# Attention beside an FFN on one core: 21 of 56 FFN1 tiles made during gelu and read from the score banks

## The chip, the cores and the metric

The kernel runs on one core of a Trainium2 chip. The time is the device time of one execution in microseconds (us); the median of several executions is compared. A core has a matrix engine (TensorE, PE), a vector engine (VectorE, DVE), an activation engine (ScalarE, ACT), a general one (GpSimd, POOL) and a queue engine (SyncE, SP), which here starts nearly all DMA transfers. Each engine works through its own list of instructions in order and waits for others by semaphores. PSUM, where matmuls write, has eight banks of 128 x 512 fp32.

## The reference

```python
x = A_x                                  # 1 x 2048 x 448
xn = _layernorm(x, axis=-1)
s = _A_ref(xn, A_wqkv, A_wo)             # attention, 16 heads of 28, softmax over 2048 keys
g = _silu(_B_ref(xn, B_w1, B_b1, B_w2, B_b2))
return x + s * g

def _B_ref(x, w1, b1, w2, b2):           # FFN, 448 -> 1792 -> 448
    h = jnp.einsum("bsd,df->bsf", x, w1) + b1
    h = _gelu(h)                         # tanh form
    return jnp.einsum("bsf,fd->bsd", h, w2) + b2
```

## The kernel before

Queries are cut into four chunks of 512 (c), heads into four groups of four (g). A block b = 4g + c is one group of heads over one chunk of queries. It has 64 score tiles of 128 keys x 512 queries, so there are 1024 tiles, numbered m. Four heads sit in four strips of 32 rows, so the score matmuls of several heads run beside each other in the array.

Six PSUM banks form the ring of scores; of the other two, `acc` gathers the weighted sums (P times V) and `misc` is the one spare bank that everything else shares, one user at a time. From block 1 on, tiles are made in units of three (in block 0, of two): `p_scores` (matmuls, line 1011) fills three banks, `p_exps` (ScalarE, line 1038) turns them into probabilities P with one instruction, and the other three banks are filled meanwhile. `p_pv` (line 1137) multiplies P with V.

Some tiles do not go to ScalarE. They are called late: their exp is computed by VectorE with a polynomial, tile by tile from the ring (line 1065), then in pairs of tiles with five instructions (`p_exp2`, lines 1089 to 1096), and they join the weighted sum when they are ready. `COUNTS` gives the number of late tiles of each of the blocks 1 to 14, and `OFFS` their places and pairing; a late tile is always the third of its unit, so that the unit's exp has two tiles.

The FFN runs beside this. FFN1 has 4 x 14 = 56 tiles of 128 x 512, each four matmuls (line 916) into the spare bank, and VectorE adds b1 while it moves the tile to `h` in SBUF (line 929). When all 56 are done, `p_gelu` puts four gelu instructions of 14 tiles each into ScalarE's list (line 941), between two loads of the activation table; scores and exps stand still for that time. FFN2 (line 959, 14 matmuls for each of 16 tiles), silu by tanh (line 973) and the output projection (line 1226) follow beside the later blocks, again over the spare bank.

The order of each engine's instructions is fixed when the program is built. A planner runs all these processes against estimated durations. Each step is a task with an engine, what it reads and writes, a duration and a priority (a lower number goes first). The planner takes the task that can start earliest, and among those within 0.1 us the one of best priority; the list of each engine is the order in which its tasks were taken. The semaphore waits follow from reads and writes. A process can wait for a condition on the plan (`"until"`) or for a free bank (`"bank"`).

Inputs are loaded through SP's queue at the start: x, the weights, b1 (line 572, 128 x 14 elements), b2, and w1. `constants` clears the padding: `xn` is 448 columns wide, padded with zeros to 512, and rows 448 to 511 of `w1` are zero (line 492).

Of the kernel before, what the change touches and what calls it, by code (L numbers as in the profile page):

```python
# [8 lines left out]
ALU = mybir.AluOpType  # L9
# [10 lines left out]
C = 4  # L20
# [11 lines left out]
OFFS = {2: ((0,), (21,)), 3: ((0, 9), (30,)), 4: ((0, 9), (21, 33)), 5: ((0, 9), (18, 27), (39,)),  # L32
        6: ((0, 9), (18, 27), (33, 39)), 7: ((0, 6), (12, 21), (27, 33), (39,))}
COUNTS = (5, 5, 4, 5, 4, 5, 4, 4, 4, 6, 6, 6, 4, 3)
for _b in range(1, NBLK - 1):
    _m = 64 * _b + 4
    while (_m - 64) % UB != UB - 1:
        _m += 1
    for _o in OFFS[COUNTS[_b - 1]]:
        _ms = tuple(_m + x for x in _o)  # L40
        LATE.update(_ms)
        for _k in _ms:
            PAIR[_k] = _ms
# [3 lines left out]
for _m in list(range(0, 64, 2)) + list(range(64, MTOT, UB)):  # L47
    _ms = list(range(_m, _m + (2 if _m < 64 else UB)))
    _b0 = _m % 4 if _m < 64 else (_m - 64) % NRING
    _na = len([m for m in _ms if m not in LATE])  # L50
    if _p + _na > NP:
        _p = 0
    UNITS.append((_ms, _ms[:_na], _b0, _p))
    for _k, m in enumerate(_ms):
        UOF[m] = len(UNITS) - 1
        RB[m] = _b0 + _k
        RPREV[m] = _last.get(RB[m])
        _last[RB[m]] = m
        if _k < _na:
            PB[m] = _p + _k  # L60
            PPREV[m] = _plast.get(PB[m])
            _plast[PB[m]] = m
    _p += _na
NU = len(UNITS)
# [5 lines left out]
PV_START = 8  # L70
SEM = 0.07
# [25 lines left out]
class _Kernel:  # L97
# [164 lines left out]
    def alloc(self):  # L262
# [28 lines left out]
        self.b1s = sb("b1s", [128, FT], bf)  # L291
        self.b1c = sb("b1c", [128, FT], f32)
# [48 lines left out]
        self.b_b1, self.b_b1c, self.b_b2 = B(), B(), B()  # L341
# [27 lines left out]
        self.s_x2 = [self.sem("s_x2%d" % q) for q in range(4)]  # L369
        self.s_x0b, self.s_wqk1 = self.sem("s_x0b"), self.sem("s_wqk1")  # L370
# [3 lines left out]
    def schedule(self):  # L374
# [28 lines left out]
        K.b1_done = False  # L403
        K.gelu_done = False
        self.constants()
# [9 lines left out]
        K.spawn(K.p_late(), 0)  # L415
        o = 1.0
# [23 lines left out]
        f1 = deque((c, ft) for c in range(C) for ft in range(FT))  # L440
        for c in range(C):
            for _ in range(6):
                K.spawn(K.p_f1(*f1.popleft()), nxt())
            K.spawn(K.p_k(2, c), nxt())
            K.spawn(K.p_q(2, c), nxt())
# [5 lines left out]
        K.spawn(K.p_gelu(), 0)  # L451
        for c in range(C):
            for t in range(4):
                K.spawn(K.p_f2(c, t), nxt())
            K.spawn(K.p_silu(c), nxt())
# [10 lines left out]
    def constants(self):  # L466
# [3 lines left out]
        def f(eng):  # L470
            eng.memset(K.epsc[:, :], LN_EPS)
            eng.memset(K.dum[:, :], 1.0)
            eng.memset(K.ones[:, :], 1.0)
            eng.memset(K.E_sb[:, :, :], 0.0)
            eng.memset(K.stg[64:128, 3, :, :, :], 0.0)
            pad = lambda w: w.rearrange("p k (h e) -> p (k h) e", e=32)[:, :, DH:32]
            eng.memset(pad(K.wq[:, :, :]), 0.0)
            eng.memset(pad(K.wk[:, :, :]), 0.0)
            eng.memset(pad(K.wsq), 0.0)
            return eng.memset(K.xn[:, :, :, D:512], 0.0)  # L480
        e(DVE, f, writes=[K.b_pads], dur=1.6)

        def late_pads():
            yield ("until", lambda: K.b_xnT[0][1].tw is not None)

            def f(eng):
                eng.memset(K.wv[64:128, 3, :], 0.0)
                eng.memset(K.wv[0:64, 3, D:WS], 0.0)
                return eng.memset(K.wv[:, 0:3, D:WS], 0.0)
            yield _Task(DVE, f, [], [K.b_wvpad], 0.4, 0.05, 1)  # L490
            yield ("until", lambda: K.ln_done == 2 * C)
            yield _Task(DVE, lambda eng: eng.memset(K.w1[64:128, 3, :], 0.0), [], [K.b_w1pad], 0.8, 0.05, 4)
        K.spawn(late_pads(), 3)
# [52 lines left out]
    def loads(self):  # L546
# [23 lines left out]
        def f(eng):  # L570
            with K.nc.allow_non_contiguous_dma(reason="tiny bias load"):
                return eng.dma_start(K.b1s[:, :], K.B_b1.rearrange("(ft p) -> p ft", p=128))
        K.dma(SP, f, K.s_w["b"], writes=[K.b_b1], land=20)
        ld(K.b2b[:, :], K.B_b2.partition_broadcast(128), K.s_w["b"], [K.b_b2], 20)
        K.b_b1.w = K.b_b2.w
# [333 lines left out]
    def p_f1(self, c, ft):  # L909
        K = self  # L910
        bank, tok = yield ("bank", lambda: K.ready(K.b_xnT[c] + [K.b_w1, K.b_w1pad, K.b_b1]) and K.stg_done == 2 and K.norms_done)
        for k in range(2):
            def f(eng, k=k):
                ins = None
                for kt in (2 * k, 2 * k + 1):
                    ins = eng.matmul(bank, K.w1[:, kt, ft * 128:(ft + 1) * 128], K.xnT[:, kt, c * 512:(c + 1) * 512],  # L916
                                     start=(kt == 0), stop=(kt == KT - 1))
                return ins
            yield _Task(PE, f, [K.b_w1, K.b_w1pad, K.b_xnT[c][k]], [tok], 0.5, 0.12)
        if not K.b1_done:  # L920
            K.b1_done = True
            yield _Task(DVE, lambda eng: eng.tensor_copy(K.b1c[:, :], K.b1s[:, :]), [K.b_b1], [K.b_b1c], 0.17)
        dst = K.h[:, c, ft * 512:(ft + 1) * 512]
        wr = [K.b_hf[c][ft]]
        if c == 3:
            for x in K.b_xn:
                for y in x:
                    wr[0].r += y.r
        yield _Task(DVE, lambda eng: eng.tensor_scalar(dst, bank, K.b1c[:, ft:ft + 1], None, op0=ALU.add),  # L929
                    [tok, K.b_b1c], wr, 0.75, 0.0, 2)  # L930
        K.banks.append((bank, tok))
        K.n_f1 += 1

    def p_gelu(self):
        K = self
        yield ("until", lambda: K.n_f1 == C * FT and K.ready([b for r in K.b_hf for b in r], 0.5))
        for c in range(C):
            hv = K.h[:, c, :]

            def f(eng, hv=hv):  # L940
                return eng.activation(hv, hv, ACTF.Gelu_apprx_tanh)  # L941
            yield _Task(ACT, f, K.b_hf[c], [K.b_h[c]], 6.15 + (1.3 if c == 0 else 0), 0.0, -1)
        K.prog[ACT].append(lambda eng: eng.preload_act_table_set("exp_and_others"))
        K.tE[ACT] += 1.3
        for b in K.b_fsb + K.b_sig:
            b.w = K.b_w1.w
            b.r = list(K.b_w1.r) + [K.b_w1pad.w]
        K.gelu_done = True

    def p_f2(self, c, t):  # L950
        K = self
        bank, tok = yield ("bank", lambda: K.ready([K.b_h[c], K.b_w2]) and (c < 2 or K.g_done[c - 2]))
# [44 lines left out]
    def p_scores(self):  # L997
        K = self
        for u in range(NU):
# [23 lines left out]
            if len(ms) == 3 and not K.ring6:  # L1023
                yield ("until", lambda: K.taken == 2)
                K.ring6 = True
            yield ("until", lambda: all(RPREV[m] is None or K.ring_rel[RPREV[m]] for m in ms))
# [3 lines left out]
    def p_exps(self):  # L1030
        K = self
        for u in range(NU):
# [11 lines left out]
            K.exp_m = UNITS[u][0][-1]  # L1044
# [4 lines left out]
    def p_late(self):  # L1049
# [5 lines left out]
        for u in range(NU):  # L1055
            for m in UNITS[u][0]:
# [13 lines left out]
                if m == PAIR[m][-1]:  # L1070
                    K.spawn(K.p_exp2(PAIR[m], i), m)

# [31 lines left out]
    def p_pv(self):  # L1104
# [5 lines left out]
        for q in range(MTOT // 4):  # L1110
# [6 lines left out]
            for m, k, half in list(K.late_ready):  # L1117
                hole = (4 * q + m % 4) in LATE and all(m % 4 != x[0] % 4 for x in late)
                if m // 64 == b and (end or len(K.late_ready) - len(late) > 3 or (hole and K.ready([K.b_pl[k]]))):
# [23 lines left out]
            def fall(eng, fl=fl):  # L1143
                ins = None
                for f in fl:
# [3 lines left out]
                        lambda: 1.2 if K.exp_u - K.pv_u > 4 else 6)  # L1149
# [167 lines left out]
```

## Time and profile before

| | |
|---|---|
| median of 7 runs | 499.02 us (497.91 to 500.77) |
| the profiled execution | 500.8 us, span of its instructions 499.0 us |
| mean granted TensorE clock | 0.958 of full |
| ScalarE busy | 475.4 us, 95% of the span |
| TensorE busy | 418.5 us, 84% |
| VectorE busy | 387.9 us, 78% |
| exps on ScalarE | 352 instructions |
| FFN1 moves on VectorE | 56, mean 747 ns |
| first and last start of gelu | 325.3 and 343.5 us |

How to read it: a group's line gives source line, engine, operation, output and input, shapes and count, then the busy time and the mean duration of one in ns, then how long the engine sat idle just before such instructions and what ended that. Durations of neighbours on an engine overlap a little, so the pitch from start to start is what counts in a sum. A row of a table by stretches gives, for each engine, its busy time and number of instructions, then the granted TensorE clock as a share of full, the DMA share and the GB/s. Four matmuls into one tile are shown as one row with x4.

### The profile page before, as it was taken

What the parts mean: (1) busy time and instruction counts of PE and PEld (TensorE: products, weight loads), DVE (VectorE), ACT (ScalarE), POOL (GpSimd) and SP (SyncE); (2) the same over time, 40 slices, a digit from 0 to 9 for tenths busy, and PEclk for the clock granted to TensorE, in tenths of its full rate; (3) what the DMA queues carried; (4) which work ended last, traced back from release to release, by engine and by line L of the source; (5) the groups of instructions that cost most, each with busy time, mean ns of one, the idle gap of its engine ahead of it and who ended that gap; (6) DMA issues with size and microseconds to landing.
All of it is one profiled execution on the core that took longest, in us unless ns stands there. A gap on an engine that the chain in (4) does not pass through costs nothing.

```text
span 499.0 us, 8625 instructions
## 1 busy us (share of the span) xinstructions
PE 418.5 (84%) x3486; PEld 140.2 (28%) x3519; DVE 387.9 (78%) x545; ACT 475.4 (95%) x382; POOL 83.7 (17%) x91
## 2 busy tenths in 40 slices
PE   6999789886998888888788888756899999998884
PEld 4442223221221222222222222211233333322342
DVE  7744998888688968997886969993297999678454
ACT  5998999999999999999999999999799999999994
POOL 6571112041210212121101001041000102010100
PEclk9998999999888999999989999985799999999999
DMA  8500000000000000001300000000001001102110
GB/s 238 146 17 19 0 1 1 0 1 3 0 1 0 1 1 0 2 1 20 111 0 1 1 1 1 1 0 0 0 2 38 2 0 37 39 0 71 43 49 30
DMA packets 10088, 11.00 MB, mean 22 GB/s; under 512 B 3456, under 2 KB 8704, under 8 KB 10048
## 3 DMA queue, kind: packets, MB, share of 16 engines
q1 hardware_dynamic: 9904, 10.21, 6.9%
q8 instruction: 28, 0.46, 0.4%
q10 hardware_dynamic: 144, 0.23, 0.1%
q14 instruction: 12, 0.10, 0.1%
HBM read 8.61 MB, written 1.84 MB: 21 GB/s over the span
## 4 chain that ended last, share of the span: by engine, by line
PE 36%; ACT 31%; issue 18%; DVE 11%; POOL 3%; DMA 1%; ACTq 0%; DVEq 0%; POOLq 0%
ACT P L1038 30%; PE ring L1011 9%; PE misc L959 7%; PE acc L1137 6%; PE misc L916 6%; PE misc L671 3%; DVE h L929 1%; POOL rlo L1202 1%; DVE x_sb L1065 1%; DVE kT L1090 1%; POOL rhi L1201 1%; ACT w L973 1%; DVE kT L682 1%; DVE kT L1089 1%; PE misc L1226 1%
## 5 line engine op out<-in xcount | busy, mean ns | idle before, releaser
L1038 ACT ACTIVATE P<-ring 128x1536 bf16<-128x1536 f32 (+1 forms) x352 | 435.3, 1433 | 11.2 <-PE ring L1011 10.3
L1011 PE MATMUL ring<-qT,kT 32*128 32x512 bf16 (+1 forms) x1216 | 139.2, 355 | 42.4 <-ACT P L1038 38.3
L1137 PE MATMUL acc<-P,vaug 128*32 128x512 bf16 (+1 forms) x1151 | 96.9, 355 | 1.0 <-ACT P L1038 0.4
L1011 PEld LDWEIGHTS ring<-qT,kT 32*128 32x128 bf16 x1216 | 36.9, 91 | 159.6 <-ACT P L1038 137.8
L916 PE MATMUL misc<-xnT,w 128*128 128x512 bf16 x208 | 61.6, 399 | 4.4 <-issue 1.8
L929 DVE TENSOR_SCALAR h<-misc,b1c 128x512 bf16<-128x512 f32 x56 | 41.8, 747 | 24.0 <-PE misc L916 23.7
L1201 POOL CAST rhi<-rc 128x512 bf16<-128x512 f32 x15 | 15.3, 1017 | 242.6 <-DVE rc L1197 216.7
L959 PE MATMUL misc<-w,h 128*128 128x448 bf16 x224 | 53.4, 364 | 2.0 <-DVE qT L852 0.9
L1065 DVE TENSOR_SCALAR x_sb<-ring 128x512 int32<-128x512 f32 x65 | 44.6, 686 | 8.9 <-PE ring L1011 8.4
L857 POOL TENSOR_TENSOR qsq<-qT 128x512 bf16<-128x512 bf16 x15 | 23.3, 1554 | 131.5 <-DVE qT L852 125.2
L1137 PEld LDWEIGHTS acc<-P,vaug 128*32 128x32 bf16 x1151 | 25.5, 94 | 56.9 <-issue 50.1
L959 PEld LDWEIGHTS misc<-w,h 128*128 128x128 bf16 x224 | 17.9, 99 | 27.5 <-issue 14.0
L916 PEld LDWEIGHTS misc<-xnT,w 128*128 128x128 bf16 x224 | 15.9, 100 | 32.0 <-issue 15.4
L941 ACT ACTIVATE h<-h 128x7168 bf16<-128x7168 bf16 x4 | 24.4, 6164 | 0.0
L671 PE MATMUL misc<-xnT,wq 128*128 128x512 bf16 x58 | 18.5, 432 | 5.8 <-DVE qT L862 3.6
L1202 POOL TENSOR_TENSOR rlo<-rc,rhi 128x512 bf16<-128x512 f32 x15 | 22.1, 1470 | 1.2
L1094 DVE SCALAR_TENSOR_TENSOR kT<-kT 128x1024 f32<-128x1024 f32 (+1 forms) x17 | 21.7, 1278 | 0.2
L1090 DVE SCALAR_TENSOR_TENSOR kT<-kT 128x1024 f32<-128x1024 f32 (+1 forms) x17 | 21.2, 1250 | 0.4
L1092 DVE SCALAR_TENSOR_TENSOR w<-w 128x1024 f32<-128x1024 f32 (+1 forms) x18 | 21.2, 1179 | 0.2
L964 DVE TENSOR_TENSOR w<-misc,b2b 128x448 bf16<-128x448 f32 x16 | 9.9, 621 | 14.3 <-PE misc L959 14.3
L1090 DVE SCALAR_TENSOR_TENSOR w<-w 128x1024 f32<-128x1024 f32 (+1 forms) x18 | 20.6, 1145 | 0.4
L1094 DVE SCALAR_TENSOR_TENSOR w<-w 128x1024 f32<-128x1024 f32 (+1 forms) x18 | 20.8, 1153 | 0.1
(135 smaller groups left out, 408.3 us busy)
## 6 DMA issues: line engine op xcount, KB each, us to landing
h<-in_A_x_dram SPq DMA_DIRECT2D x4, 448.0 KB, 3.3
w<-in_B_w_dram SPq DMA_DIRECT2D x1, 1568.0 KB, 7.4
x_sb<-in_A_x_dram SPq DMA_DIRECT2D x3, 448.0 KB, 5.8
w<-in_B_w_dram SPq DMA_DIRECT2D x1, 1344.0 KB, 7.8
out_dram<-h SPq DMA_DIRECT2D x6, 224.0 KB, 1.9
h<-in_A_wqkv_dram SPq DMA_DIRECT2D x3, 168.0 KB, 5.9
out_dram<-h SPq DMA_DIRECT2D x4, 112.0 KB, 1.7
wo<-in_A_wo_dram SPq DMA_DIRECT2D x16, 24.5 KB
```

Of the source, the lines that this page charges most:

```text
L671: ins = eng.matmul(bank, w[:, kt, g * 128:(g + 1) * 128], K.xnT[:, kt, c * 512:(c + 1) * 512], start=(kt == 0), stop=(kt == KT - 1))
L916: ins = eng.matmul(bank, K.w1[:, kt, ft * 128:(ft + 1) * 128], K.xnT[:, kt, c * 512:(c + 1) * 512], start=(kt == 0), stop=(kt == KT - 1))
L929: yield _Task(DVE, lambda eng: eng.tensor_scalar(dst, bank, K.b1c[:, ft:ft + 1], None, op0=ALU.add), [tok, K.b_b1c], wr, 0.75, 0.0, 2)
L941: return eng.activation(hv, hv, ACTF.Gelu_apprx_tanh)
L959: ins = eng.matmul(ps, hv[:, ft, t * 128:(t + 1) * 128], K.w2[:, ft, :], start=(ft == 0), stop=(ft == FT - 1))
L1011: return eng.matmul(K.ring[:, RB[m], col:col + nq], K.kT[32 * j:32 * j + 32, g, t * 128:(t + 1) * 128], K.qT[32 * j:32 * j + 32, g, c * 51 ...
L1038: return eng.activation(K.P[:, p0:p0 + n, :], K.ring[:, b0:b0 + n, :], ACTF.Exp, scale=SM_SCALE)
L1065: yield _Task(DVE, lambda eng, m=m, i=i, half=half: eng.tensor_scalar(K.ysb[i][:, 512 * half:512 * half + 512], K.ring[:, RB[m], :], SM_SC ...
L1090: yield _Task(DVE, lambda eng: eng.scalar_tensor_tensor(u, v, EXP_A, v, op0=ALU.add, op1=ALU.mult), [tv], [tu], d1, 0.0, 4)
L1094: yield _Task(DVE, lambda eng: eng.scalar_tensor_tensor(u, v, EXP_D, u, op0=ALU.mult, op1=ALU.add), [tv, tu], [tu], d1, 0.0, 4)
L1137: return eng.matmul(K.acc[32 * j:32 * j + 32, q0:q0 + nq], K.vaug[:, t, 4 * g + j, :], ap[:, col:col + nq], tile_position=(0, 32 * j), sta ...
L1202: yield _Task(En, lambda eng: eng.tensor_tensor(K.rlo[:, :, :], rcb, K.rhi[:, :, :], ALU.subtract), [K.b_rc, K.b_rhl], [K.b_rhl], d2, 0.0, 1)
```

## The change

- Only 35 of the 56 FFN1 tiles (`SBT`) go through the spare bank and VectorE to `h` in SBUF. The other 21 (`DIRECT`, seven trios) are made while gelu runs, straight into the three ring banks that are free, and gelu reads them there: `p_direct` makes them, `p_gelu` now has 15 pieces (`PIECES`), alternating between SBUF and ring. Its place is fixed at the first unit that reaches tile 6 of block 9 (`GU`, unit 204). The scores of the unit after next wait in the plan until the last trio is read.
- b1 becomes row 448 of w1. A column of ones in the padding of `xn` multiplies it, so the move to SBUF is a plain copy. The row is loaded after the padding of w1 is cleared.
- Four pairs of tiles of block 9 (`MPAIRS`) leave the units; their scores go through the spare bank to VectorE (`p_mlate`). All in all 76 tiles instead of 65 are late.
- The tables of late tiles are counted in units now, and the last unit has one tile. The weighted sum takes a late tile only once it is ready, and it goes ahead of other work around the start of gelu. Each chunk's first four FFN1 tiles, not six, come before its projections for group 2.

```diff
-OFFS = {2: ((0,), (21,)), 3: ((0, 9), (30,)), 4: ((0, 9), (21, 33)), 5: ((0, 9), (18, 27), (39,)),
...
-COUNTS = (5, 5, 4, 5, 4, 5, 4, 4, 4, 6, 6, 6, 4, 3)
...
+COUNTS = (5, 4, 5, 4, 5, 5, 5, 6, 1, 6, 6, 6, 6, 4)
+GM = 64 * 9 + 6
+MPAIRS = [tuple(64 * 9 + x for x in p) for p in ((16, 21), (26, 31), (36, 41), (46, 51))]
...
+_seq = [m for m in range(64, MTOT) if m not in MLATE]
+_US = [list(range(m, m + 2)) for m in range(0, 64, 2)] + [_seq[i:i + UB] for i in range(0, len(_seq), UB)]
+GU = min(u for u, ms in enumerate(_US) if ms[-1] >= GM)
...
+DIRECT = [(2, 5), (2, 8), (2, 11), (3, 0), (3, 3), (3, 6), (3, 9)]
+PIECES = [(0, 0, 5), None, (0, 5, 5), None, (0, 10, 4), None, (1, 0, 5), None, (1, 5, 5), None, (1, 10, 4), None,
+          (2, 0, 5), None, (3, 12, 2)]
+SBT = [(c, ft) for c, f0, n in [p for p in PIECES if p] for ft in range(f0, f0 + n)]
...
-        f1 = deque((c, ft) for c in range(C) for ft in range(FT))
+        f1 = deque(SBT)
         for c in range(C):
-            for _ in range(6):
+            for _ in range(4):
                 K.spawn(K.p_f1(*f1.popleft()), nxt())
...
-            return eng.memset(K.xn[:, :, :, D:512], 0.0)
+            eng.memset(K.xn[:, :, :, D + 1:512], 0.0)
+            return eng.memset(K.xn[:, :, :, D:D + 1], 1.0)
...
+            K.dma(SP, lambda eng: eng.dma_start(K.w1[64:65, 3, :], K.B_b1.rearrange("(o f) -> o f", o=1)), K.s_b1,
+                  writes=[K.b_w1pad], land=K.now + 4)
...
-                return eng.dma_start(K.b1s[:, :], K.B_b1.rearrange("(ft p) -> p ft", p=128))
...
-        yield _Task(DVE, lambda eng: eng.tensor_scalar(dst, bank, K.b1c[:, ft:ft + 1], None, op0=ALU.add),
-                    [tok, K.b_b1c], wr, 0.75, 0.0, 2)
+        yield _Task(DVE, lambda eng: eng.tensor_copy(dst, bank), [tok], wr, 0.69, 0.0, 2)
...
+    def p_direct(self):
+        K = self
+        s0 = UNITS[GU - 1][2]
+        for i, (c, f0) in enumerate(DIRECT):
+            b0 = (s0 + 3 * i) % NRING
+            yield ("until", lambda: K.exp_u >= GU - 1 + i if i < 2 else K.dir_read >= i - 1)
+            for n in range(3):
+                for k in range(2):
+                    yield K.t_f1(c, f0 + n, K.ring[:, b0 + n, :], K.b_ring[b0 + n], k, 3.5)
+            K.dir_n += 1
 
     def p_gelu(self):
         K = self
-        yield ("until", lambda: K.n_f1 == C * FT and K.ready([b for r in K.b_hf for b in r], 0.5))
-        for c in range(C):
-            hv = K.h[:, c, :]
...
+        yield ("until", lambda: K.exp_u >= GU and K.n_f1 == len(SBT))
...
+        for q, pc in enumerate(PIECES):
+            if pc:
+                c, f0, n = pc
+                src = K.h[:, c, 512 * f0:512 * (f0 + n)]
...
+                src = K.ring[:, b0:b0 + 3, :].rearrange("p b n -> p (b n)")
...
+            yield _Task(ACT, lambda eng, dst=dst, src=src: eng.activation(dst, src, ACTF.Gelu_apprx_tanh), rd,
+                        K.b_hf[c][f0:f0 + n] + ([K.b_h[c]] if left[c] == 0 else []),
+                        0.4267 * n + (0.12 if pc else 0.085) + (1.3 if q == 0 else 0), 0.05, -1)
...
+            if u == GU + 1:
+                yield ("until", lambda: K.dir_read == len(DIRECT))
...
+    def p_mlate(self):
+        K = self
+        yield ("until", lambda: K.exp_u >= GU - 1)
+        for ms in MPAIRS:
+            yield ("until", lambda: len(K.ys) > 0)
+            i = K.ys.pop(0)
+            for half, m in enumerate(ms):
+                bank, tok = yield ("bank",)
...
-                if m // 64 == b and (end or len(K.late_ready) - len(late) > 3 or (hole and K.ready([K.b_pl[k]]))):
+                if m // 64 == b and (end or (K.ready([K.b_pl[k]]) and (hole or len(K.late_ready) - len(late) > 3))):
...
-                        lambda: 1.2 if K.exp_u - K.pv_u > 4 else 6)
+                        lambda: 1.2 if K.exp_u - K.pv_u > 4 or GU - 1 <= K.exp_u <= GU else 6)
```

## The prediction

> **What bounds the kernel now.** I read the page's busy shares first, then ScalarE's own timeline, then the granted clock stretch by stretch, and last the groups by form, for durations.
>
> ```profile
> PE 418.5 (84%) x3486; PEld 140.2 (28%) x3519; DVE 387.9 (78%) x545; ACT 475.4 (95%) x382; POOL 83.7 (17%) x91
> L1038 ACT ACTIVATE P<-ring 128x1536 bf16<-128x1536 f32 (+1 forms) x352 | 435.3, 1433 | 11.2 <-PE ring L1011 10.3
> ```
>
> ScalarE (ACT) is busy 95% of the span. From its first exp at 13.4 us to its last at 492.7 it has only 11.2 us of idle before exps, and nearly all of that waits for scores from TensorE (PE). So the time is ScalarE's work plus those waits. Only three things count: fewer or shorter ScalarE instructions, smaller waits, and the tail after the last exp.
>
> The chain of waits gives the pitch of the exps from their start times:
>
> ```profile
> 395.38 0.86 ACT P L1038
> 396.29 0.76 ACT P L1038
> 397.62 2.15 ACT P L1038 x2
> ```
>
> A three-tile exp takes 1.33 us start to start, a two-tile one 0.91. The difference, 0.42, is one tile (512 elements); each instruction then carries about 0.05 more. A one-tile exp is 0.48.
>
> Now gelu, in ScalarE's timeline:
>
> ```profile
> 324.04 1.28 ACT L941 ACT_TABLE_LOAD   x1
> 325.33 24.38 ACT L941 ACTIVATE h<-h 128x7168 bf16<-128x7168 bf16 x4
> 349.73 1.28 ACT L943 ACT_TABLE_LOAD   x1
> 351.02 2.37 ACT L1038 ACTIVATE P<-ring 128x1024 bf16<-128x1024 f32 x2
> 356.13 2.54 ACT L1038 ACTIVATE P<-ring 128x1536 bf16<-128x1536 f32 x2 [2.74 <-PE ring L1011]
> 359.47 2.79 ACT L1038 ACTIVATE P<-ring 128x1536 bf16<-128x1536 f32 x2 [0.80 <-PE ring L1011]
> ```
>
> Four gelus of 14 tiles take 24.4 us: 56 x 0.427 = 23.9, so 0.1 us is fixed in each. The scores are not ready afterwards: 2.74 + 0.80 = 3.54 us of waits, a third of all there are. The windows say why (busy us of PE, PEld, DVE, ACT, POOL, then the clock):
>
> ```profile
> 324.00:336.00 12.00, 6.28 (x44) 2.26 (x44) 12.00 (x15) 11.97 (x4) 4.52 (x4) 0.92 0.00 0
> 336.00:351.00 15.00, 9.27 (x23) 2.19 (x21) 5.39 (x8) 14.98 (x4) 2.43 (x2) 0.50 0.00 0
> ```
>
> TensorE has little to do during gelu: 23 matmuls in 15 us, each projection waiting for the one spare bank to be emptied. Its clock is halved, and an FFN2 tile of 14 matmuls (4.43 us at half clock) then stands ahead of the scores.
>
> **The change part by part.**
>
> *Exps.* Late tiles (exp on VectorE, DVE) go from 65 to 76, counted from the two tables of the code. ScalarE's units go from 255 threes and 97 twos to 249 threes, 100 twos and a single: -6 x 1.33 + 3 x 0.91 + 0.48 = **-4.8 us**.
>
> *Gelu in 15 pieces.* 56 tiles remain: 8 pieces from SBUF (35 tiles), 7 from the score banks (21). Gelu from PSUM is not in the trace. The nearest row is the exp from the same banks, 0.05 fixed; the SBUF gelus show 0.10, and no row shows a tile below 0.427. That is 8 x 0.10 + 7 x 0.05 = 1.15 against 0.4 now: **+0.75 us** (ends +0.7 and +1.1).
>
> *FFN1 tiles made during gelu.* 84 matmuls. Their two rates:
>
> ```profile
> 341.63 1.89 PE L671 MATMUL misc<-xnT,wq 128*128 128x512 bf16 x4 [0.84 <-DVE kT L682]
> 262.99 1.04 PE L916 MATMUL misc<-xnT,w 128*128 128x512 bf16 x4
> ```
>
> Less the last one's own latency (0.63 and 0.38) that is 0.42 us apart at half clock, 0.22 at full. A trio of tiles is 12 matmuls, 2.64 us at full clock. ScalarE reads a trio every 1.33 + 2.23 (five SBUF tiles) = 3.56 us, or 3.1 where the SBUF piece has four. The first trio starts one exp (1.33) and a table load (1.28) before gelu and is wanted only after another 2.23: 4.8 us for 2.64 of work. At full clock there is 0.5 to 0.9 us to spare per trio for the catching-up weighted sums, the eight spare-bank scores and the projections: no stall, cost **0**, with TensorE's own speed as the cover. If that goes, rival 1 prices it.
>
> *Restart.* The scores of the unit after next wait for the seventh trio to be read. Behind that read ScalarE still has a two-tile SBUF gelu (0.95) and a table load (1.28), and scores take 0.39. With a TensorE that has been busy and is at full clock, the 3.54 us of waits go: **-3.5 us** (ends 0 and -3.5). Next late are the FFN2 chunks in front of scores, as everywhere after 356 us.
>
> *Clock rule.* By the Trainium skill ("TensorE: Matmul & The Clock Gate", Part 1) the clock halves after an idle window of about 3.4 us and recovers after a busy one. This trace is harsher:
>
> ```profile
> 120.00:124.00 4.00, 2.06 (x17) 0.62 (x18) 3.46 (x5) 4.00 (x4) 0.00 (x0) 0.82 0.02 6
> 124.00:128.00 4.00, 3.62 (x18) 0.87 (x18) 1.35 (x2) 3.06 (x4) 0.00 (x0) 0.50 0.01 2
> ```
>
> Half-busy with no gap over 0.75 us, it was halved, and ScalarE lost 0.94 + 0.22 us when an FFN1 tile came at that clock. The rule alone would leave the stretch after FFN2's end at full clock: +0. The trace says scores and weighted sums alone (just the load of 120 to 124) halve it. With gelu some 57 us earlier FFN2 ends earlier too, so such a stretch appears near 390 to 450 us. In 123 to 125.5 half clock alone cost ScalarE nothing; the output projections and normalisations in it would. I take **+1 us** (ends 0 and +5: 12 output tiles at 0.4).
>
> *Gelu's place.* It moves to unit 204, about 268 us in this trace. 35 tiles must be out by then:
>
> ```profile
> 110.00:256.00 146.00, 23.91 (x32) 0.94 0.04 12
> 110.00:268.00 158.00, 27.65 (x37) 0.95 0.04 11
> ```
>
> 37 bias-adds of FFN1 had started by 268 us, with all projections of group 2 done as well; 35 by about 263. Cost 0, with some 4 us of cover.
>
> *VectorE.* 11 more score reads x 0.69, five more pairs at 0.75 + 1.30 + 1.28 + 1.27 + 1.22 = 5.8, one single 3.2: +40. Minus 21 bias-adds of 0.747, and 35 that become copies (0.747 to the 0.687 of the same-shape cast): -18. So +22 us, 388 to 410 of 490. Only two of the eleven tiles fall before gelu; eight are taken in and after it, where DVE is idle 9.6 of 15 us. Hidden.
>
> *b1.* The 0.17 us cast that sat ahead of the first bias-add goes. The row is a 3.5 KB transfer that must follow the pad memset at 24.9 us; the old b1 load took 6.5 us to land, and first use is at 117 us. On SP it stands in a queue that waits for GpSimd's wo memset until 33.3 us anyway. GpSimd's queue is not passed. The fourth K chunk has always been 128 rows, so no matmul is added. Cost 0.
>
> *Pad memset.* The column of ones makes the zero run 63 wide. The trace has 384 words in 0.38 us (line 480). The Trainium skill ("VectorE: DVE Perf Modes", Zero memsets can be issued as uint32) says an odd count of bf16 has no word form: 756 elements, 0.75 us by the row's rate, against 0.38 if it were not so. It would end near 3.4; statistics begin at 3.86 when x lands. +0 on the path either way.
>
> *Tail.* 32 weighted-sum matmuls (0.89 us) end the work behind the last exp; with a single tile last, 16 are left (0.41): **-0.4**.
>
> Sum: -4.8 + 0.75 - 3.5 + 1.0 - 0.4 = -6.95. The profiled execution took 500.8 us (span 499.0, 1.8 around it), 0.4% above the median of 499.02, so I lay the difference on the median: **492.0 us**.
>
> **The rivals.**
>
> *1. TensorE bounds gelu (slower).* Place: the seven trios. At half clock a trio is 12 x 0.42 + 0.2 = 5.25 us against 3.56. The seventh would be ready 36.8 us after the first's start, and is wanted at 4.8 + 6 x 3.5 = 25.8: ScalarE loses 11 us, 503 us. It decides from a spacing of about 0.28 us per matmul, or from 0.9 us of other work or of waits for the spare bank per trio, since PE's queue is in order and a spare-bank score waits for VectorE, which works in 1.3 us steps. For: the clock in this stretch today. Against: the cause of that is idleness, the clock was 1.00 from 256 to 270, and 12 dense matmuls per trio are the load that brings it back. Chance 0.16.
>
> *2. A cold TensorE after FFN2.* The +5 end above, and normalisations on top: 496 to 498. For: the 120 us rows. Against: from 464 to 472 us PE is 74% busy and stays at 1.00. Chance 0.12.
>
> *3. Gelu waits for FFN1.* Two more late tiles on VectorE ahead of it (7 us) could set FFN1 back by three tiles, at about 2.5 us each: 7.5 us, less the cover, given back: 496 to 499.5. Against: VectorE waited 23.7 us for those tiles, not they for it. The edit then does not do what it says, since the next unit's scores are held until gelu is through. Chance 0.10.
>
> **How the numbers follow.** The likeliest case, 0.62, gives 492 (489 to 495 by the ends above and a few half-clock windows more or less). Rival 2 at 0.12 and 3 at 0.10 lie mostly below the median; rival 1 at 0.16 above. 0.3%, about what this measurement can tell from no change, is 1.5 us. Faster 0.74, same 0.08, slower 0.18. The range 488 to 500.5 leaves out rival 1 and the far ends.
>
> **What would show it.** Right: gelu's 15 pieces and two table loads in about 28 us without waits for PE; clock 1.00 in that stretch; no wait over 0.5 at the restart; ACT busy near 471; DVE near 410. Wrong: ScalarE idle before gelu pieces, released by PE (rival 1); new waits before exps with a clock of 0.5 between FFN2's end and the last block (2); ScalarE idle before the first table load (3).

## The result and the profile after

The changed kernel takes 495.22 us (median of 12 runs, 493.68 to 497.28) against 499.65 (median of 31 runs of before). The ratio is 0.9918, with a 95% interval of 0.9902 to 0.9933: faster by 0.8%. The forecast was 492.0, in a range of 488 to 500.5. The sign is right, and 4.4 us came instead of 7.

One profiled execution of each is compared below. After's took 494.87 us (span 493.1), before's 500.8 (span 499.0): the spans differ by 5.9.

From the page of after, the busy shares and the group of the exps:

```profile
PE 421.6 (86%) x3489; PEld 143.6 (29%) x3519; DVE 407.2 (83%) x565; ACT 470.7 (95%) x391; POOL 83.8 (17%) x91
L1087 ACT ACTIVATE P<-ring 128x1536 bf16<-128x1536 f32 (+1 forms) x350 | 430.1, 1446 | 8.7 <-PE ring L1058 8.2
```

ScalarE works 470.7 us instead of 475.4, and the idle time ahead of exps falls from 11.2 to 8.7. VectorE takes the load, 407.2 instead of 387.9. It is still ScalarE that sets the time.

ScalarE's timeline around gelu, with the ring and SBUF pieces in turn:

```profile
263.73 1.28 ACT L985 ACT_TABLE_LOAD   x1
265.03 2.34 ACT L985 ACTIVATE h<-h 128x2560 bf16<-128x2560 bf16 x1
267.27 1.43 ACT L985 ACTIVATE h<-ring 128x1536 bf16<-128x1536 f32 x1
268.60 2.33 ACT L985 ACTIVATE h<-h 128x2560 bf16<-128x2560 bf16 x1
...
290.21 1.28 ACT L990 ACT_TABLE_LOAD   x1
291.50 8.25 ACT L1087 ACTIVATE P<-ring 128x1536 bf16<-128x1536 f32 x6
300.35 1.02 ACT L1087 ACTIVATE P<-ring 128x1024 bf16<-128x1024 f32 x1 [0.60 <-PE ring L1058]
302.19 2.79 ACT L1087 ACTIVATE P<-ring 128x1536 bf16<-128x1536 f32 x2 [0.81 <-PE ring L1058]
```

No bracket stands at any of the 15 pieces: none waited. The first gelu starts at 265.03 and the table load behind the last at 290.21, so gelu takes 25.18 us against 24.40 before. Six exps then run without a wait. The 2.74 + 0.80 us of waits at the restart have become 0.60 + 0.81, some nine us behind it.

The windows (busy us of PE, PEld, DVE, ACT, POOL, then the granted clock) over gelu and where the waits now are:

```profile
264.00:272.00 8.00, 7.84 (x44) 3.10 (x44) 7.46 (x9) 7.99 (x5) 0.00 (x0) 1.00 0.00 0
288.00:296.00 8.00, 5.17 (x27) 0.99 (x27) 7.16 (x10) 7.97 (x7) 1.95 (x1) 0.72 0.00 1
296.00:304.00 8.00, 7.53 (x45) 1.72 (x42) 6.17 (x9) 6.58 (x6) 0.00 (x0) 0.64 0.00 0
392.00:400.00 8.00, 5.36 (x38) 1.24 (x39) 7.17 (x8) 8.00 (x8) 0.00 (x0) 0.62 0.00 0
400.00:408.00 8.00, 7.76 (x41) 1.90 (x32) 5.93 (x7) 6.23 (x5) 1.66 (x2) 0.53 0.20 59
```

The direct tiles keep TensorE at full clock through gelu, where before had 0.50. Half-clock stretches follow once they end: around 291 to 302 us, 394 to 408, 455 to 466, and again in the last microseconds; one of 3.4 us lies before gelu, near 112. ScalarE's column shows the loss in each second row: 6.58 and 6.23 of 8 us busy.

The difference of the spans has three parts. The first exp starts 0.35 later (13.75 against 13.40); from first exp to the end of the last it is 472.24 us against 479.34, -7.1; and what follows the last exp is 7.11 against 6.25, +0.86. The sum is -5.9.

Why only -4.4 between the medians: runs of one program differ by how long its clock was halved. Over the 62 runs of before that stand beside experiments 1 to 10 (median 499.01) a straight line through time and mean clock loses 0.23 us per 0.001 of clock; over the 12 runs of after it is 0.20 (0.941 gave 497.1 and 497.3, 0.958 gave 493.7). 0.001 of a mean over some 495 us is about 1 us at half clock, so such a microsecond costs about 0.2 us. At a clock of 0.955 the two lines stand at 500.55 and 494.62, 5.9 apart, as the profiles do. But before's median clock is 0.9615 and after's 0.9535, and 0.008 at that rate is 1.6 us. TensorE is colder in the changed kernel, and that shows in the medians, not in the pair of profiles, whose clocks were 0.958 and 0.955. It is a correlation between runs of one program. That it also holds from one program to another is not shown: the kernel of experiment 1 below is colder than after and waits less.

### The profile page after: what moved, and what is told of

It reads as the page before. It is cut to its first block, busy times and chain, and to the rows that moved or that the text cites. A ratio compares the mean times of both kernels' runs of the same rounds, so it can differ in the third digit from the quotient of the medians.

```text
span 493.1 us, 8661 instructions
## 1 busy us (share of the span) xinstructions
PE 421.6 (86%) x3489; PEld 143.6 (29%) x3519; DVE 407.2 (83%) x565; ACT 470.7 (95%) x391; POOL 83.8 (17%) x91
## 4 chain that ended last, share of the span: by engine, by line
ACT 44%; PE 30%; issue 19%; DVE 5%; POOL 1%; POOLq 0%; ACTq 0%; DVEq 0%
ACT P L1087 40%; PE ring L1058 8%; PE acc L1206 6%; PE misc L1006 6%; ACT h L985 3%; PE misc L685 2%; PE misc L1295 2%; PE acc L798 1%; PE misc L948 1%; PE ring L948 1%; DVE x_sb L1114 1%; DVE w L1159 1%; PE misc L890 1%; PE ring L890 1%; ACT w L1020 1%
## 5 line engine op out<-in xcount | busy, mean ns | idle before, releaser
L1087 ACT ACTIVATE P<-ring 128x1536 bf16<-128x1536 f32 (+1 forms) x350 | 430.1, 1446 | 8.7 <-PE ring L1058 8.2
L1206 PE MATMUL acc<-P,vaug 128*32 128x512 bf16 (+1 forms) x1140 | 100.0, 366 | 1.3 <-issue 0.7
L1270 POOL CAST rhi<-rc 128x512 bf16<-128x512 f32 x15 | 17.1, 1143 | 233.8 <-DVE rc L1266 233.8
L1114 DVE TENSOR_SCALAR x_sb<-ring 128x512 int32<-128x512 f32 x68 | 46.6, 685 | 11.7 <-PE ring L1058 10.9
L948 PE MATMUL misc<-xnT,w 128*128 128x512 bf16 x128 | 35.8, 382 | 3.3 <-issue 1.6
L1165 DVE SCALAR_TENSOR_TENSOR x_sb<-x_sb,kT 128x1024 uint16<-128x1024 int32 (+1 forms) x22 | 28.2, 1280 | 0.3
L931 DVE CAST h<-misc 128x512 bf16<-128x512 f32 x35 | 24.0, 686 | 5.1 <-PE misc L948 4.8
L1163 DVE SCALAR_TENSOR_TENSOR kT<-kT 128x1024 f32<-128x1024 f32 (+1 forms) x22 | 27.5, 1252 | 0.3
L1159 DVE SCALAR_TENSOR_TENSOR kT<-kT 128x1024 f32<-128x1024 f32 (+1 forms) x22 | 26.9, 1224 | 0.3
L1161 DVE SCALAR_TENSOR_TENSOR kT<-kT 128x1024 f32<-128x1024 f32 (+1 forms) x22 | 26.5, 1202 | 0.3
L1165 DVE SCALAR_TENSOR_TENSOR x_sb<-x_sb,w 128x1024 uint16<-128x1024 int32 (+1 forms) x19 | 21.1, 1113 | 0.1
L948 PE MATMUL ring<-xnT,w 128*128 128x512 bf16 x82 | 19.8, 381 | 1.2 <-ACT h L985 1.0
```

The source lines that it names most:

```text
L931: yield _Task(DVE, lambda eng: eng.tensor_copy(dst, bank), [tok], wr, 0.69, 0.0, 2)
L1087: return eng.activation(K.P[:, p0:p0 + n, :], K.ring[:, b0:b0 + n, :], ACTF.Exp, scale=SM_SCALE)
L1114: yield _Task(DVE, lambda eng, m=m, i=i, half=half: eng.tensor_scalar(K.ysb[i][:, 512 * half:512 * half + 512], K.ring[:, RB[m], :], SM_SC ...
L1159: yield _Task(DVE, lambda eng: eng.scalar_tensor_tensor(u, v, EXP_A, v, op0=ALU.add, op1=ALU.mult), [tv], [tu], d1, 0.0, 4)
L1161: yield _Task(DVE, lambda eng: eng.scalar_tensor_tensor(u, u, EXP_B, u, op0=ALU.add, op1=ALU.mult), [tu], [tu], d1, 0.0, 4)
L1163: yield _Task(DVE, lambda eng: eng.scalar_tensor_tensor(u, v, EXP_D, u, op0=ALU.mult, op1=ALU.add), [tv, tu], [tu], d1, 0.0, 4)
```

## The experiments

The theory of the prediction is that fewer exps and a fed TensorE make the gain, and that a thin or late TensorE takes some of it back; each expectation names the theories that its run tells apart. Unless said otherwise an experiment is an edit of the changed kernel, and ratios are to the kernel before on the same chip. The edits of experiments 3, 4, 8 and 9 are shown shortened.

**1. The changed kernel with the old number of late tiles.**

```diff
-COUNTS = (5, 4, 5, 4, 5, 5, 5, 6, 1, 6, 6, 6, 6, 4)
-MPAIRS = [tuple(64 * 9 + x for x in p) for p in ((16, 21), (26, 31), (36, 41), (46, 51))]
+COUNTS = (5, 5, 4, 5, 4, 5, 4, 4, 4, 6, 6, 6, 4, 3)
+MPAIRS = [tuple(64 * 9 + x for x in p) for p in ()]
```

> The changed kernel with 65 late tiles as before (the four pairs of block 9 back in the units, the old counts per block), so only the trios and the b1 row are left of the change. Theory A (the eleven exps fewer carry the gain, 4.8 us; the waits 2.5): about 499 to 500, that is 495.2 plus 4.8, less up to 1 because VectorE has 40 us less to do. Theory B (the busy TensorE during gelu and the smaller waits carry it): 495 to 496.

Measured: 498.49 us, ratio 0.9986 (0.9963 to 1.0008), span 495.5. So 65 late tiles leave a gain that can't be told from none. ScalarE's waits by line:

```profile
ACT P L1087 <- PE ring L1058: 6.8, 12, 1.5
```

ScalarE is back at 475.7 us busy, 5.0 more than after, but its waits are 1.4 us smaller than after's, and VectorE is at 370.6. ScalarE restarts behind gelu without any wait at full clock:

```profile
290.10 1.28 ACT L990 ACT_TABLE_LOAD   x1
291.39 10.00 ACT L1087 ACTIVATE P<-ring 128x1536 bf16<-128x1536 f32 x8
```

So without its extra late tiles the change removes the whole 3.54 us of the restart, as the prediction had it; the 1.41 that after shows there come with the late tiles. Gelu's earlier place and the new order of the weighted sums around it are in this too, and no run parts them from the direct tiles. The fewer exps are worth 3.3 us in medians, not 4.8. In the profiles this kernel's span is 2.4 us longer than after's: 5.0 of ScalarE's work, less 1.4 of waits, 1.0 behind the last exp (its last unit is a three again) and 0.3 at the start. Its median clock, 0.9405, is lower than after's, and its waits are smaller.

**2. The kernel before with 76 late tiles**, and nothing else.

```diff
-COUNTS = (5, 5, 4, 5, 4, 5, 4, 4, 4, 6, 6, 6, 4, 3)
+COUNTS = (6, 6, 5, 6, 5, 6, 5, 5, 5, 6, 6, 6, 5, 4)
```

> The kernel before with 76 late tiles and nothing else changed (counts 6,6,5,6,5,6,5,5,5,6,6,6,5,4). Theory A': the exps can go only because the trios relieve VectorE; without that VectorE (388 busy + 40 = 428 us) becomes late with FFN1 and with the reads of late tiles, and waits before exps eat the 4.8: 498 to 503. Theory B': VectorE has room anyway, and 495 comes out without any trio.

Measured: 525.71 us, ratio 1.0536 (1.0490 to 1.0581). Both theories missed by far. From its page and its waits:

```profile
PE 437.3 (83%) x3519; PEld 141.0 (27%) x3519; DVE 418.8 (80%) x586; ACT 470.9 (89%) x382; POOL 83.1 (16%) x91
```

```profile
ACT P L1038 <- PE acc L1137: 16.7, 8, 3.8
ACT P L1038 <- PE ring L1011: 11.2, 12, 3.5
```

ScalarE saves its 4.5 us here too. But eight times an exp waits for a weighted sum, 16.7 us in all: the probabilities' buffers stay in use because the weighted sum waits for a late tile that VectorE hasn't finished. That is about half of the 27.7 us by which its span is longer. The other half lies at the end: after the last exp ends, at 505.7 us, 21.0 us follow, 14.8 more than before. VectorE's and TensorE's timelines there:

```profile
504.15 0.62 DVE L976 SCALAR_TENSOR_TENSOR h<-w 128x448 bf16<-128x448 bf16 x1
```

```profile
509.13 3.28 PE L1226 MATMUL ring<-wo,qT 128*128 128x448 bf16 x16
516.65 0.63 PE L1137 MATMUL acc<-P,vaug 128*32 128x128 bf16 x32
```

The last silu product is made at 504 us (in after at 460), and the output projections that need it come after the last exp, ahead of the last weighted sum. VectorE is busy only 80% of the span, yet ScalarE and TensorE wait for it in the stretches that count. So the eleven tiles are not free to move. The change differs from this kernel in three ways that can make them cheap: where they are placed, the 17.8 us by which FFN1's moves get shorter (41.8 us before, 24.0 after), and the rule that the weighted sum takes a late tile only once it is ready, which is just what it waits for here. No run tells the three apart. This table of counts is one choice; a better spread over the old kernel was not tried.

**3. and 4. TensorE's room during gelu.** One, or four, extra matmuls of 128 x 512 ahead of each of the 21 direct tiles, whose results are overwritten.

```diff
+for _ in range(XTRA):    # 1, then 4
+    eng.matmul(bank, K.ident[:, :], K.xnT[:, 0, c * 512:(c + 1) * 512], start=True, stop=True)
 (first matmuls of the direct tile)
```

> The changed kernel with one extra matmul ahead of each directly made tile (three per trio, 0.66 us at full clock), overwritten at once; order of all lists the same. Theory A (0.5 to 0.9 us of room per trio at full clock): ScalarE waits at most 0.5 us in all during gelu, 495 to 496. Theory B (TensorE is nearly the bound in gelu): each trio later by 0.6, some 3 us in all, 498.

> The same with four extra matmuls per tile, twelve per trio: 24 x 0.22 = 5.3 us per trio, about what a trio would take at half clock. Theory A (rival 1's arithmetic): the seventh trio is ready at 37 us and wanted at 25.8, so ScalarE waits 11 us in gelu: 506. Theory B (there is slack that the sum left out): under 3 us of waits, below 498.

Measured: 496.25 us (0.9949, 0.9931 to 0.9967) with one, 510.15 (1.0232, 1.0195 to 1.0269) with four. The waits of the gelu pieces, with one and then with four:

```profile
ACT h L993 <- PE ring L949: 0.8, 2, 0.5
ACT h L993 <- PE misc L1271: 0.4, 1, 0.4
```

```profile
ACT h L993 <- PE ring L949: 11.5, 6, 2.8
ACT h L993 <- PE misc L1271: 3.0, 1, 3.0
```

Three extra matmuls per trio (0.66 us at full clock) cost 1.2 us in all seven; twelve (2.64) cost 14.5, all seven pieces from the ring waiting. The first is at the edge, the second is rival 1 made real: 14.5 us where the prediction's sum had 11. Twelve matmuls over seven trios are 18.5 us; less the room of 0.5 to 0.9 us per trio that is 12 to 15, so the room stands. The clock was 1.00 over gelu with either.

**5. The pad memset as words.** Two columns of ones instead of one, so that the zeros are 62 wide; row 449 of w1 is zero, and the second column adds nothing.

```diff
-            eng.memset(K.xn[:, :, :, D + 1:512], 0.0)
-            return eng.memset(K.xn[:, :, :, D:D + 1], 1.0)
+            eng.memset(K.xn[:, :, :, D + 2:512], 0.0)
+            return eng.memset(K.xn[:, :, :, D:D + 2], 1.0)
```

> The changed kernel with two columns of ones (the second meets zero rows of the weights) so that the zeros are 62 wide and can be cleared as words. Theory A: the first exp starts at 13.4 us as before instead of 13.75, since the 37 warm-up matmuls and the transposes behind them in TensorE's list wait for the memset: 0.35 us less, 494.9. Theory B: the later start has another cause (transfers): first exp stays at 13.7, 495.2.

Measured: 494.34 us (0.9891, 0.9855 to 0.9928). The start of the timeline, of after and then of this kernel (the trace names xn's memory h):

```profile
2.67 0.69 DVE L496 MEMSET h<- 128x756 bf16 x1
3.56 4.64 PE L798 MATMUL acc<-E_sb,ident 128*128 128x256 bf16 x21 [3.56 <-POOL tcol L526]
8.00 0.69 PE L758 MATMUL ring<-ident,h 128*128 128x128 bf16 x8
```

```profile
2.59 0.37 DVE L496 MEMSET h<- 128x372 uint32 x1
3.14 4.64 PE L798 MATMUL acc<-E_sb,ident 128*128 128x256 bf16 x21 [3.14 <-DVE h L497]
7.57 0.66 PE L758 MATMUL ring<-ident,h 128*128 128x128 bf16 x8
```

The warm-up matmuls stand at the head of TensorE's list and come after the memset; the transposes of x stand behind them. So the memset moves the first transposes (8.00 to 7.57) and the first exp (13.75 to 13.43). This is the rule of the Trainium skill ("VectorE: DVE Perf Modes", Zero memsets can be issued as uint32) seen at both sizes: 0.69 us as 756 bf16, 0.37 as 372 words. The bracket in after's line names GpSimd's `tcol`, but GpSimd's work ran at the same times in both kernels; only the memset moved, and the warm-up with it. The size varies with how long the warm-up then takes: the nine profiles here with 756 bf16 start it at 3.56 to 3.57 us and the first exp at 13.26 to 14.01 (median 13.75), the five with words at 3.12 to 3.15 and 13.40 to 13.47. The whole-run difference to after, 0.9 us (4 runs), is more than this explains and lies within the intervals; about 0.3 of it is shown.

**6. The last four tiles as 2 + 2 instead of 3 + 1**, alone and with the words of experiment 5.

```diff
+_US[-2:] = [_US[-2][:2], _US[-2][2:] + _US[-1]]
```

> The changed kernel with its last four tiles in two units of two instead of three and one; ScalarE's work is the same. Theory A (the tail of 7.1 us is TensorE's arrears: with a last exp of only 0.5 us the sums of the units before and the output projection are still in its list): the tail falls to 6.2 us or less, the last exp ends as before or 0.1 later: 494.5. Theory B (the tail is the half clock at the very end, whatever the units): tail stays at 6.3 to 7.1 with the clock, 495.

> The changed kernel with both the word-wide pad memset and the last four tiles as two and two. If both pay, 0.3 at the start and 0.7 at the end: 494; if the end doesn't, 494.6 to 495.

Measured: 495.47 us (0.9936, 0.9913 to 0.9959) and 494.35 (0.9914, 0.9884 to 0.9945): no difference to after and to experiment 5. The end of TensorE's timeline, of after, of the 2 + 2 kernel, of experiment 7 (the units of after, full clock at the end), and of before:

```profile
483.14 1.67 PE L1295 MATMUL misc<-wo,qT 128*128 128x448 bf16 x4
...
486.18 0.74 PE L1295 MATMUL ring<-wo,qT 128*128 128x448 bf16 x3
486.85 0.41 PE L1206 MATMUL acc<-P,vaug 128*32 128x128 bf16 x16
```

```profile
483.86 1.30 PE L1296 MATMUL ring<-wo,qT 128*128 128x448 bf16 x3
485.09 1.04 PE L1207 MATMUL acc<-P,vaug 128*32 128x128 bf16 x32
```

```profile
493.60 0.74 PE L1295 MATMUL ring<-wo,qT 128*128 128x448 bf16 x3 [0.39 <-ACT P L1087]
494.27 0.41 PE L1206 MATMUL acc<-P,vaug 128*32 128x128 bf16 x16
```

```profile
491.46 0.93 PE L1226 MATMUL ring<-wo,qT 128*128 128x448 bf16 x4
492.32 0.89 PE L1137 MATMUL acc<-P,vaug 128*32 128x128 bf16 x32
```

Seven output projections of the block before stand ahead of the last weighted sum. At full clock they take 0.93 + 0.74 us; in after the first four fell into half clock (1.67), in the 2 + 2 kernel the other three as well (1.30), and so the rest ends behind the last exp. The 2 + 2 kernel ends its last exp 1.55 us sooner, 484.44 against 485.99, but its span is only 1.0 shorter; 1.1 of the 1.55 are waits before gelu, where both have the same lists, so they belong to the run and not to the edit. The time after the last exp is 7.1 to 7.7 us where some of these seven run at half clock (after and experiments 5, 6, 9 and 11) and 6.1 to 6.5 where none does (before and experiments 1, 3, 4, 7, 8 and 10), whatever the size of the last unit; experiment 2 is apart.

**7. The silu products sooner.** In 388 to 403 us TensorE has no FFN2 tile, the clock halves, and two of the silu products of the chunk before stand in VectorE's list behind late exps. Their priority goes up.

```diff
-                        [K.b_sig[c % 2], K.b_fsb[c % 2]], [K.b_h[c], K.b_g[c]], 0.63, 0.0, 6)
+                        [K.b_sig[c % 2], K.b_fsb[c % 2]], [K.b_h[c], K.b_g[c]], 0.63, 0.0, 3.9)
```

> The changed kernel with VectorE's four products per chunk that end silu ahead of the late exps (priority 3.9 instead of 6). Theory A: in the changed kernel FFN2 of the last chunk waits from 388 to 403 us for these products, which stand behind late exps; TensorE runs dry, its clock halves from 393.9 to 407.5, and 2.4 us of waits before exps follow; with the products earlier these go: 493. Theory B: VectorE is simply full; the late exps become late instead and as much is lost elsewhere: 495.

Measured: 502.65 us, ratio 1.0071 (1.0046 to 1.0095): slower. FFN2 did move, the last tanh from 429.6 to 413.6 us. But the waits now read:

```profile
ACT P L1087 <- PE ring L1058: 10.2, 13, 2.2
ACT P L1087 <- PE acc L1206: 5.9, 3, 4.2
```

The weighted sums now hold up exps, as in experiment 2, where they waited for late tiles. So putting one kind of VectorE work ahead of the other loses more than it gains after gelu.

**8. A busier TensorE.** One extra matmul ahead of the scores of eight units behind gelu and of the units of the last four blocks, to hold the clock up.

```diff
+if GU < u <= GU + 8 or m0 >= 64 * 12:
+    eng.matmul(K.ring[:, RB[m0], :], K.ident[:, :], K.xnT[:, 0, 0:512], start=True, stop=True)
 (scores of the unit)
```

> The changed kernel with one extra 128x512 matmul ahead of each unit's scores for the eight units after gelu and in blocks 12 to 15, overwritten at once. Theory A (half clock is what makes these waits and the long tail): clock 1.0 there, waits before exps from 8.7 to about 4 us, tail after the last exp from 7.1 to 6.2 us: 490 to 492. Theory B (the clock has little to do with it; the extra matmuls only delay the scores by 0.22 us): 495 to 497.

Measured: 502.70 us, ratio 1.0063 (1.0037 to 1.0089). Its mean clock is 0.975, and it is slower for all that:

```profile
ACT P L1090 <- PE ring L1058: 13.2, 25, 1.5
```

The clock was still halved in 296 to 304 and in 400 to 408 us (0.63 and 0.57), and the extra matmuls stand ahead of scores that ScalarE waits for. So this run holds the clock at full in only some of the places where it was meant to, and tests the clock only in part.

**9. The kernel before, with eight extra matmuls ahead of each projection of group 3**, the work between whose waits TensorE's clock was halved during gelu.

```diff
+        if g == 3 and k == 0:
+            for _ in range(8):
+                eng.matmul(bank, w[:, 0, g * 128:(g + 1) * 128], K.xnT[:, 0, c * 512:(c + 1) * 512], start=True, stop=True)
         (the projection's matmuls)
```

> The kernel before with eight extra matmuls ahead of each projection of group 3, into the same bank and overwritten at once, so that TensorE is busy during gelu. Theory A: the restart waits of 3.5 us are the half clock; the granted clock in gelu goes to 1.0 and the waits under 1 us: about 496.5. Theory B: the waits come from the FFN2 tile that stands ahead of the scores whatever the clock: 499 to 500.

Measured: 509.22 us, ratio 1.0183 (1.0134 to 1.0231). ScalarE's timeline behind gelu, and the clock there:

```profile
365.72 2.54 ACT L1043 ACTIVATE P<-ring 128x1536 bf16<-128x1536 f32 x2 [14.34 <-PE ring L1016]
```

```profile
354.00:362.00 8.00, 5.88 (x25) 2.25 (x25) 1.80 (x3) 0.00 (x0) 1.04 (x1) 1.00 0.01 2
```

At full clock ScalarE waits 14.34 us: the scores stand in TensorE's list behind a row of projections, each of which waits for the spare bank, and the longer row moved them back. It doesn't isolate the clock, since it changed the row as well. It does show that the place of the scores in the list decides the restart, and that a full clock doesn't make up for it.

**10. The silu products on GpSimd**, in two instructions each, so that VectorE has 16 fewer.

```diff
-            yield _Task(DVE, lambda eng, t=t: eng.scalar_tensor_tensor(K.g_sb[:, c, t, :], sg[:, t, :], 1.0, fb[:, t, :],
-                                                                       op0=ALU.add, op1=ALU.mult),
...
+            yield _Task(POOL, lambda eng, t=t: eng.tensor_tensor(sg[:, t, :], sg[:, t, :], fb[:, t, :], ALU.mult),
...
+            yield _Task(POOL, lambda eng, t=t: eng.tensor_tensor(K.g_sb[:, c, t, :], sg[:, t, :], fb[:, t, :], ALU.add),
```

> The changed kernel with silu's closing products on GpSimd, as two operations each (about 1.1 us) instead of one on VectorE, which is spared 10.8 us after gelu. Theory A (VectorE, full after gelu, is what holds up FFN2 and so halves the clock): FFN2 of the last chunk follows without the gap from 388 to 403 us, the waits of 2.4 us at 400 to 409 go, perhaps those at 300 too: 492 to 493. Theory B (the waits come from the planned order of TensorE's list, not from VectorE's load): 495.

Measured: 500.92 us, ratio 1.0045 (1.0024 to 1.0065). Its page, and VectorE's timeline in a stretch in which GpSimd works and then doesn't:

```profile
PE 422.4 (85%) x3489; PEld 144.4 (29%) x3519; DVE 408.0 (82%) x549; ACT 471.6 (94%) x391; POOL 131.2 (26%) x123
```

```profile
394.29 1.93 DVE L1161 SCALAR_TENSOR_TENSOR kT<-kT 128x1024 f32<-128x1024 f32 x1
395.22 1.89 POOL L1026 TENSOR_TENSOR h<-w 128x448 bf16<-128x448 bf16 x1
...
398.23 1.93 DVE L1165 SCALAR_TENSOR_TENSOR kT<-kT 128x1024 f32<-128x1024 f32 x1
...
406.69 1.23 DVE L1161 SCALAR_TENSOR_TENSOR kT<-kT 128x1024 f32<-128x1024 f32 x1
407.95 1.22 DVE L1163 SCALAR_TENSOR_TENSOR kT<-kT 128x1024 f32<-128x1024 f32 x1
```

VectorE has 16 instructions (10.3 us) fewer and is as busy as in after, 408.0 against 407.2. Its polynomial instructions take up to 1.93 us instead of 1.23 while GpSimd works beside them, and the one-input conversion ahead of them takes 1.52 instead of 0.68. The five groups of them over this buffer sum to 135.6 us here and 125.1 in after: +10.5, all that was taken away. The Trainium skill says so ("SBUF — State Buffer", Who interferes with whom): a VectorE instruction with two SBUF inputs contends with a GpSimd instruction that reads SBUF. Relief of VectorE has to come from fewer operations, as with b1, not from GpSimd.

This run also bears on the clock. Here it was 1.00 over 392 to 408 us, and ScalarE still waited 1.15 + 0.34 + 0.67 + 0.50 us between 398 and 407, no less than after's 0.39 + 1.38 + 0.59 around its half clock. What held the scores up here was FFN2 ahead of them in TensorE's list, which waited 1.71 us for VectorE, and a score bank that VectorE had yet to read (1.19 us).

**11. Three instead of four pairs over the spare bank.** In after VectorE takes the spare-bank scores one by one beside gelu and after it, and each next one waits for the bank.

```diff
-MPAIRS = [tuple(64 * 9 + x for x in p) for p in ((16, 21), (26, 31), (36, 41), (46, 51))]
+MPAIRS = [tuple(64 * 9 + x for x in p) for p in ((16, 21), (26, 31), (36, 41))]
```

> Three instead of four pairs of tiles of block 9 go over the spare bank; 74 tiles are late, and the count of units then ends in a three. ScalarE gets 250 threes and 100 twos in place of 249 threes, 100 twos and a single: +1.33 - 0.48 = +0.85 us. Theory A (the spare-bank pairs, which VectorE works off one by one, thin TensorE's list out after gelu, and that brings the 0.60 + 0.81 us of waits there back): with two of the eight tiles gone the waits between 291 and 304 us shrink to under 0.5 us in all, and the granted clock of 296 to 304 us rises from 0.64 to 0.9 or more; together with an ending unit of three (no output projections behind a short last exp, -0.4) the time is 494.5 to 495.5. Theory B (they come from the projections that stand in TensorE's list ahead of the scores there): the waits stay at 1.2 to 1.6 us and the clock under 0.75, and the time is 495.7 to 496.5.

Measured: 496.98 us, ratio 0.9949 (0.9917 to 0.9981). The windows behind gelu:

```profile
288.00:296.00 8.00, 4.71 (x37) 1.69 (x38) 7.60 (x9) 7.97 (x7) 2.15 (x2) 1.00 0.00 1
296.00:304.00 8.00, 6.70 (x51) 1.95 (x49) 7.25 (x11) 8.00 (x7) 1.95 (x1) 1.00 0.00 0
```

The first theory was right about the place: the half clock and both waits behind gelu are gone. It was wrong about the time. Waits for scores are 9.2 us in all, against 8.2 in after: they came back at 359 to 377 us (1.04, 0.72, 1.12 and 0.16, again with a half-clock stretch), and TensorE ended at half clock. A stretch that is mended hands its thin spot to another.

Two versions stand a little below the changed kernel, experiment 5 (494.34) and experiment 6 with its words (494.35); the intervals overlap with after's.

## Why the prediction was right, and where it was off

- *Exps, -4.8.* In the trace: exps on ScalarE 430.1 us against 435.3, -5.2. Right as work saved. By experiment 1 it is 3.3 in medians: with the extra late tiles come more waits, and with the single last tile a longer end.
- *Gelu in 15 pieces, +0.75.* 25.18 against 24.40 us: +0.78. Taking the exp from the same banks as nearest row held: the ring pieces start 1.33 us before the next instruction, as three-tile exps do.
- *FFN1 trios, 0.* Right. No piece waited, the clock was 1.00, and experiments 3 and 4 put the edge where the sum had it.
- *Restart, -3.5, and colder TensorE, +1.0.* The net of the two, -2.5, is what the waits show (11.2 to 8.7), but their places are not those forecast, and that the sum agrees is in part luck. Of the waits for scores, before has 6.6 us before gelu, 3.5 at the restart and 0.2 behind; after has 3.1, 1.4 and 3.6. The fall before gelu was in no term, and it pays for what appears behind. Part of it can be the run: ten profiles with after's lists up to gelu have 2.0 to 5.7 us there, two with before's have 6.6 and 5.2. The change without its extra late tiles does take the whole 3.54 away (experiment 1). In after 1.41 return some nine us behind gelu, so "no wait over 0.5 at the restart" was wrong; they go when one spare-bank pair is taken out (experiment 11). At 401 to 409 us, behind a gap in FFN2 and not after its end, 2.36 appear.
- *VectorE, +22 and hidden.* The size was 19.3 (387.9 to 407.2), near enough. By the tables three of the eleven tiles, not two, fall before gelu. "Hidden" was too easy: up to gelu it is, but afterwards late exps and silu products are in each other's way (experiments 7 and 10), and what they delay is TensorE's work. Experiment 2 shows what as many late tiles can cost without the rest of the change.
- *Pad memset, +0.* The failed step. The cover that was named, x's landing at 3.86 us, hides it from VectorE's statistics; TensorE's warm-up waited for it too, with the transposes behind. It measured +0.35 in this pair of profiles (experiment 5 takes 0.32 of it back). The question left out was who else waits for the memset.
- *Tail, -0.4.* The second failed step: +0.86. The single last tile does halve the last weighted sum, 0.89 to 0.41 us. But before's 0.89 did not all lie behind the last exp: they began at 492.32 us, that exp ended at 492.74, so only 0.47 were left and there was nothing to gain. In after, three output projections stand between the last two sums, and a last exp of 0.60 us no longer covers them: in experiment 7, at full clock, 0.64 us of them and the sum are left behind the last exp, in after, partly at half clock, 1.27.
- *Laid on the median.* The measured terms above make -5.7, the spans differ by 5.9, and the medians by 4.4: 495.22 us lies just above the 489 to 495 of the likeliest case. The profiled pair had nearly the same clock; the runs don't (0.9615 and 0.9535). If the slope of the runs holds between the two kernels, the colder TensorE that the prediction counted as +1.0 in the profile is another 1.6 us in the medians. That would be rival 2 at a smaller size, beside the likeliest case and not instead of it. Rival 1 did not happen, and rival 3 did not: gelu started without a wait for FFN1.

What stays open is whether half clock by itself costs the waits. Apart from 1.7 us in the first 46 us, the waits of after for scores lie in or behind half-clock stretches, and runs lose about 0.2 us per microsecond of them. Against that, experiments 8, 9 and 10 had waits at full clock, where something stood ahead of the scores in TensorE's list, and experiment 1 was colder than after with smaller waits. A thin TensorE list may make both; no run here held the list and changed the clock alone.

## What to carry to other kernels

Ask of every instruction that gets longer who waits for it on all engines, also in the first 4 us: the warm-up of another engine was the one that counted. Moving work to an engine that is 78% busy is cheap only where that engine is not already the one that later steps wait for; check the stretch, not the share, and don't count on GpSimd to relieve VectorE if both read SBUF. When a sum of waits comes out as forecast, compare their places too. And before laying a difference of two profiles on a median, look how clock and time go together over the runs of both kernels: a pair with equal clocks can hide what a change does to the clock.

## What the runs showed of the hardware that was not expected

- Beside GpSimd instructions that read SBUF, VectorE's two-input instructions of 128 x 1024 took up to 1.93 us instead of 1.23 (experiment 10), and the work taken from VectorE came back in full.
- For one and the same program, each microsecond at half clock went with about 0.2 us of time: 0.23 over 62 runs of before, 0.20 over 12 of after. Between programs this need not hold.
- The clock halved with TensorE 5.17 to 5.36 us of 8 busy (288 to 296 and 392 to 400 us of after), and stayed full with 4.71 of 8 (288 to 296 us of experiment 11). The busy share over 8 us doesn't tell the two apart.
